# Second chunk's attention in float32 beside the first chunk's first stage, and a reordered opening, in a fused attention and two-MLP kernel

## The chip, the cores and the metric

One core of a Trainium2 chip. The metric is device microseconds (us) of one execution; the time before is the median of three runs. Engines are named as in the profile: PE (TensorE), DVE (VectorE), ACT (ScalarE), POOL (GpSimd), SP (SyncE, which issues most DMAs).

## What is computed

Attention over 4 batches, 8 heads, 576 positions and 64 dimensions, followed by two MLPs of 512 to 2048 to 512 over the 2304 resulting rows. Half of the heads see a local window of 32 positions, half see every 32nd position:

```
scores = where(mask, q @ k.T / 8, -1e9)
attn = exp(scores - max); attn = attn / (sum(attn) + 1e-9)
x = (attn @ v) laid out as [2304, 512]
h = x @ w_in;  x = (h * sigmoid(1.702 h)) @ w_out
h = x @ w2_in; out = (h * sigmoid(h)) @ w2_out
```

q, k and v are float32. The four weights are float64 and are turned into float32 on the chip.

## The kernel before

**Chunks.** The sequence is cut into 8 chunks of 288 positions, two for each batch (an even chunk c has s = 0, an odd one s = 1). For each chunk there is an attention (four head pairs: scores, exponentials, transposes, then two products with v that write x) and the first MLP, in two stages: 16 first-stage tiles (x times a tile of w_in, then gelu) and 64 second-stage steps (times w_out). A first program covers chunks 0 to 6 and the attention of chunk 7; a second covers chunk 7's first MLP and all of the second MLP.

**Precision.** Most products are made of three half-precision products: each operand is scaled and split into a high and a low half (`hi_lo`, L390 high half on ACT or POOL, L395 low half on DVE). The scale needs sums of squares (`square`, L494 on ACT or L496 on DVE, summed by PE at L409). Chunk 0 is the exception: its attention and its MLP run in float32 matmuls without splits, since the weights aren't split yet. A float32 matmul appears in the trace as two instructions.

**Weights.** `convert` (L426) takes a 512 KB float64 tile by DMA (L276, SP's queue) into one of eight landing places or two spare buffers, makes two ACT passes for the parts of the bit pattern (L434, L281), one ACT pass for the sign (L285, into a PSUM bank), one DVE pass (L289) and one POOL addition (L294). Then PE adds the tile to a norm (L302). There are 16 tiles of w_in (into regA) and 16 of w_out (into regB). First-stage tile f of chunk 0 (L829) needs tile f of w_in, second-stage step f (L859) needs tile f of w_out. After chunk 0 has used a tile it is split in place for the later chunks (L832 and L863 are their two stages).

**Order.** All of this is a list of tasks with engines, estimated costs, buffers and a due time (the smaller, the earlier). `Planner.run` plays the list against its own model of engines and one DMA link and fixes the order of instructions on every engine; an engine takes the ready task with the smallest due time, and one that needs another activation table only if none without a switch is due within 24. On the chip the order stands, and each engine waits in it. Chunk 0's MLP is due from 28 (T0), chunk 1's from 86 (T1); the attention of chunk c has its due times relative to the start of chunk c-1 (ATT0 for chunk 0, relative to 0; ATT1 for chunk 1, relative to 28). Weight tile i of w_in is due for loading at 3.0 + 1.9 i, of w_out at 34.0 + 1.9 i.

**Chunk 1 before.** Its q and k are loaded, squared together with chunk 0's k, scaled, and q, both k and v are split; the scores (L681), due from 54, use half-precision operands (kh, qh), and the products with v (L756) use vz and split probabilities (ptt; L720 and L723). There is one buffer each for q (rq), v (rv) and x, two for k (rk).

**Opening before.** Ahead of the plan stand the identity, the masks (mk, made by POOL), the clearing of rv (L348 to L350 on DVE) and of parts of rk. The plan loads chunk 0's q in two DMAs (L567, L568), its k in two (L551, L552), then its v in six (L589), all from SP.

## Time and profile before

| | |
|---|---|
| median of three runs | 862.29 us (859.1 to 863.71) |
| the profiled execution | 863.66 us, of it 861.9 us span |
| PE busy | 817.2 us (95%) |
| DVE, ACT, POOL busy | 629.1 us (73%), 528.2 us (61%), 394.6 us (46%) |
| DMA | 156.86 MB, 182 GB/s over the span |
| chain that ended last | PE 59%, DVE 13%, DMA 9%, ACT 7%, POOL 6%, issue 4% |

The span runs from the first to the last instruction. The chain follows the work that ended last back to its start; "issue" is time in which an engine waited for nothing that the profile shows. In a timeline, a bracket gives the idle time of the engine ahead of the instruction and what ended it. The granted clock is a share of the full 2.4 GHz; its other level is 1.2 GHz.

### The profile page before, as it was taken

The page shows a single profiled execution, that of the slowest core. Times are in us where ns is not written, and L with a number is a line of the kernel's source. Part 1 is how long each engine was busy: PE and PEld are TensorE (multiplying, and loading weights), DVE is VectorE, ACT ScalarE, POOL GpSimd, SP SyncE. Part 2 cuts the span into 40 slices and gives each one's busy share as a digit, 9 for nine tenths or more (in the row PEclk, how much of TensorE's full clock was granted, in tenths as well). Part 3 has the DMA queues.
Part 4 walks back from the last instruction along what each step waited for, and adds up shares of the span by engine and source line. Part 5 has one row for each costly group of instructions (what it writes and reads, how often), then busy time and mean ns, then how long its engine had stood idle before and what let it go on. Part 6 is the DMA issues. An engine that isn't in the chain of part 4 may idle for free.

```text
span 861.9 us, 25035 instructions
## 1 busy us (share of the span) xinstructions
PE 817.2 (95%) x10278; PEld 681.4 (79%) x10278; DVE 629.1 (73%) x1141; ACT 528.2 (61%) x970; POOL 394.6 (46%) x398
## 2 busy tenths in 40 slices
PE   2698899999999998999999999999999999999997
PEld 1575677777788776887878878888889998888886
DVE  5536899965787858988473455879888799878742
ACT  1778878677879569986572434454555576646510
POOL 2638873442442435654321343778877553222110
PEclk9999999999999999999999999999999999999999
DMA  7977724156476386773221652676766889756501
GB/s 163 277 251 208 206 78 133 38 154 183 146 218 221 112 250 200 238 229 115 64 94 36 263 199 83 212 227 223 234 202 217 297 297 307 238 172 233 185 25 50
DMA packets 90227, 156.86 MB, mean 182 GB/s; under 512 B 9032, under 2 KB 48784, under 8 KB 90112
## 3 DMA queue, kind: packets, MB, share of 16 engines
q1 hardware_dynamic: 90112, 155.26, 56.5%
q8 instruction: 80, 1.31, 0.7%
q14 instruction: 35, 0.29, 0.1%
HBM read 101.74 MB, written 53.48 MB: 180 GB/s over the span
## 4 chain that ended last, share of the span: by engine, by line
PE 59%; DVE 13%; DMA 9%; ACT 7%; POOL 6%; issue 4%; SPq 1%; DVEq 0%; POOLq 0%; ACTq 0%
PE aps L1143 9%; PE aps L1254 8%; PE hps L1143 5%; PE gps L1143 4%; PE hps L1254 4%; PE gps L1254 4%; PE aps L863 4%; PE gps L863 3%; DMA rv<-in_v_dram 2%; PE aps L832 2%; DMA regB<-in_moe_w_in_dram 1%; PE gps L1006 1%; PE aps L987 1%; DVE jv L496 1%; DVE regA L395 1%
## 5 line engine op out<-in xcount | busy, mean ns | idle before, releaser
L1143 PEld LDWEIGHTS <-wf 128*128 128x128 f16 x1680 | 150.6, 98 | 15.3
L1254 PEld LDWEIGHTS <-wf 128*128 128x128 f16 x1512 | 147.6, 98 | 18.6 <-issue 1.1
L832 PEld LDWEIGHTS <-regA 128*128 128x128 f16 x1152 | 112.4, 98 | 29.6 <-issue 0.5
L863 PEld LDWEIGHTS <-regB 128*128 128x128 f16 x1152 | 110.6, 99 | 28.0 <-DVE regB L395 0.7
L959 POOL TENSOR_TENSOR tt<-tt 128x256 f32<-128x256 f32 (+2 forms) x84 | 75.7, 912 | 44.0 <-DVE wf L966 11.5
L294 POOL TENSOR_TENSOR wm<-wm 128x512 int32<-128x512 int32 x32 | 43.2, 1349 | 84.6 <-DVE wm L289 66.3
L863 PE MATMUL aps<-g,regB 128*128 128x288 f16 x576 | 78.7, 289 | 0.0
L954 ACT ACTIVATE wf<-tt,xsg 128x512 f16<-128x512 f32 x87 | 58.1, 713 | 27.1 <-PE hps L1254 7.5
L832 PE MATMUL aps<-x,regA 128*128 128x288 f16 x552 | 73.5, 286 | 0.1
L966 DVE SCALAR_TENSOR_TENSOR wf<-tt,xsg,wf 128x512 f16<-128x512 f32 x87 | 70.5, 858 | 0.0
L863 PE MATMUL gps<-g,regB 128*128 128x288 f16 x480 | 64.7, 287 | 0.0
L703 POOL TENSOR_TENSOR prt<-prt,sus 128x378 f32<-128x378 f32 x32 | 28.3, 889 | 58.7 <-DVE sus L702 51.1
L1254 PE MATMUL aps<-regA,wf 128*128 128x256 f16 x456 | 53.2, 273 | 0.1
L1143 PE MATMUL aps<-xfa,wf 128*128 128x256 f16 (+1 forms) x528 | 53.1, 256 | 0.0
L832 PE MATMUL hps<-x,regA 128*128 128x288 f16 x312 | 42.5, 286 | 0.0
L1155 ACT ACTIVATE tt<-tt 128x512 f32<-128x512 f32 x39 | 24.4, 625 | 28.5 <-DVE tt L1150 28.4
L832 PE MATMUL gps<-x,regA 128*128 128x288 f16 x288 | 39.1, 286 | 0.0
L1143 PE MATMUL aps<-g,wf 128*128 128x256 f16 x324 | 38.8, 273 | 0.0
L954 ACT ACTIVATE wf<-regB,xsg 128x512 f16<-128x512 f32 x39 | 27.1, 715 | 18.2 <-DMA regB<-g_scratch 7.0
L1254 PE MATMUL aps<-regB,wf 128*128 128x256 f16 x312 | 37.0, 273 | 0.0
L1254 PE MATMUL hps<-regA,wf 128*128 128x256 f16 x264 | 32.4, 273 | 0.8 <-DVE x L1269 0.5
L966 DVE SCALAR_TENSOR_TENSOR wf<-regB,xsg,wf 128x512 f16<-128x512 f32 x39 | 32.5, 856 | 0.0
(324 smaller groups left out, 1889.7 us busy)
## 6 DMA issues: line engine op xcount, KB each, us to landing
tt<-g_scratch SPq DMA_DIRECT2D x76, 256.0 KB
g_scratch<-tt SPq DMA_DIRECT2D x64, 256.0 KB
w<-in_moe_w_out_dram SPq DMA_DIRECT2D x24, 512.0 KB
regB<-in_moe_w_in_dram SPq DMA_DIRECT2D x16, 512.0 KB
w<-in_moe_w_in_dram SPq DMA_DIRECT2D x16, 512.0 KB
w_scratch<-wm SPq DMA_DIRECT2D x32, 256.0 KB
regB<-g_scratch SPq DMA_DIRECT2D x32, 256.0 KB
wf<-in_factors SPq DMA_DIRECT2D x8, 896.0 KB
```

The lines of the kernel that those rows point to most:

```text
L294: nc.gpsimd.tensor_tensor(out=di, in0=m.bitcast(I32), in1=di, op=ALU.add)
L395: dve_t(n), prio, lambda on: nc.vector.scalar_tensor_tensor(out=lo(), in0=src(), scalar=s(), in1=hi(), op0=ALU.mult, op1=ALU.subtract),
L496: nc.vector.scalar_tensor_tensor(out=jv[:, 0:n], in0=src(), scalar=1.0, in1=src(), op0=ALU.mult, op1=ALU.mult, accum_out=out)
L703: kno = P.add({"POOL": 1.0}, t + 8, lambda on: nc.gpsimd.tensor_tensor(out=sets(N), in0=sets(N), in1=wide(sus[:, sl.idx], 2 * NLB), op=ALU ...
L832: nc.tensor.matmul(o, lhsT=pvA[:, f, x, kk, :], rhs=x1[:, y, kk, :], start=(i == 0), stop=(i == 3 * KD - 1))
L863: nc.tensor.matmul(o, lhsT=pvB[:, f, u, dt * 128:(dt + 1) * 128], rhs=g1[:, w, f, :], start=(f == 0 and j == 0), stop=(f == KF - 1 and j = ...
L954: nc.scalar.activation(out=out, in_=in_, func=AF.Copy, scale=s)
L959: return P.add({e: x for e, x in any_add(n).items() if e in by}, prio, lambda on: (nc.gpsimd if on == "POOL" else nc.vector).tensor_tensor ...
L966: dve_t(n), prio, lambda on: nc.vector.scalar_tensor_tensor(out=lo(), in0=src(), scalar=s(), in1=hi(), op0=ALU.mult, op1=ALU.subtract),
L1143: nc.tensor.matmul(place(b, f), lhsT=wf[:, nf * g + f, x, wa, 128 * kk:128 * kk + 128], rhs=rhs.rearrange("p (h t) -> p h t", h=2) if n2 = ...
L1155: return P.add(act_t(512), t + 5, lambda on: nc.scalar.activation(out=sl(b), in_=sl(b), func=AF.Silu), after, (), [b], tab="silu")
L1254: nc.tensor.matmul(bank(b)[:, 256 * half:256 * half + 256], lhsT=fb[:, x, a, 128 * f:128 * f + 128], rhs=wt[:, 4 * p + f, z, wi, :], start ...
```

## The change

1. Chunk 1's scores and products with v use float32 operands straight from rq, rk and rv, as chunk 0's do. Gone for chunk 1: the squares of q and of both k, the splits of q, both k and v, the split of the probabilities. The squares of v stay and give one scale for x (`small("x1s", ...)`), applied where x is written.
2. Its due times move: load of q and k from 36 to 29, of v from 41 to 37, scores from 54 to 38, products with v from 70 and 84 to 68 and 71. The products with v also wait for all of chunk 0's first-stage tiles, and chunk 1's first-stage tiles for all converted tiles of w_out.
3. Chunk 0's q and k are loaded ahead of everything else, in eight DMAs, half of them issued by ACT: heads 0 and 1 first, then heads 2 and 3. The identity follows them.
4. Chunk 0's v is due for loading at 7.3 in place of 1.0, behind weight tiles 0 to 2 (3.0, 4.9, 6.8).
5. A third of rv's clearing moves from DVE to ACT; an exponential ahead of it loads that table. The planner starts with that table, counts DMA from 2.0 on, and lets no first ACT pass of a w_in tile begin before 13.
6. The strided half of k lies behind the zeros in rk and not ahead of them; chunk 0's products with v are due at 19.2 and 21.0; the reciprocal is due at t + 5.1 in place of t + 7 in every chunk.

The core of the diff:

```diff
+ACT_AT = 13.0
-ATT0 = {"load": (0.0, 1.0), "s": 5.0, "step": 1.5, "av": (12.0, 14.0)}
-ATT1 = {"load": (8.0, 13.0), "square": (14.0, 18.0), "scale": 19.0, "split": (20.0, 21.0, 28.0), "s": 26.0, "step": 6.0,
-        "av": (42.0, 56.0)}
+ATT0 = {"load": (0.0, 7.3), "s": 5.0, "step": 1.5, "av": (19.2, 21.0)}
+ATT1 = {"load": (1.0, 9.0), "square": (0.0, 20.0), "scale": 24.0, "s": 10.0, "step": 6.0, "av": (40.0, 43.0)}
...
-        events, n, link = [], itertools.count(), t
+        events, n, link = [], itertools.count(), t + self.FIRST
...
+    for h in range(0, 4, 2):
+        nq, nk = slice(h * HS, (h + 2) * HS), slice(h * (32 + HS), (h + 2) * (32 + HS))
+        nc.sync.dma_start(out=rq[0:64, nq], in_=q[0][:, nq])
+        nc.scalar.dma_start(out=rq[64:128, nq], in_=q[0][:, NQ:2 * NQ][:, nq])
+        nc.sync.dma_start(out=rk[0:64, 0, nk], in_=k[0][:, nk])
+        nc.scalar.dma_start(out=rk[64:128, 0, KO:NK][:, nq], in_=k[0][:, NK:NK + NQ][:, nq])
...
-    nc.vector.memset(rv[96:128], 0.0)
+    nc.scalar.activation(out=tot[:, 0, 0:1], in_=ones[:, 0:1], func=AF.Exp)
+    nc.scalar.activation(out=rv[96:128].rearrange("p n h d -> p (n h) d"), in_=ones[96:128, None, 0:D].to_broadcast([32, 4 * NV, D]),
+                         func=AF.Copy, scale=0.0)
...
-            out=wm[:, m.idx], in_=raw()[:, :, 1].bitcast(F32), func=AF.Copy, scale=REBIAS), [k0], [m, *dtakes], rb)
+            out=wm[:, m.idx], in_=raw()[:, :, 1].bitcast(F32), func=AF.Copy, scale=REBIAS), [k0], [m, *dtakes], rb, at=act_at)
...
-            sq = [square(c, b + tab["square"][0], NQ, 0, lambda: rq, [kq], [rqb]),
+            sq = [*([square(c, b + tab["square"][0], NQ, 0, lambda: rq, [kq], [rqb])] if c > 1 else []),
...
+        if c > 1:
             qhb, vzb = P.buf("qh"), P.buf("vz")
...
-            if c == 1:
-                split_k(0, b + tab["split"][1])
...
-                            qx = (qh[rows, y] if c else rq[rows])[:, HS * i:HS * i + HS]
+                            qx = (qh[rows, y] if c > 1 else rq[rows])[:, HS * i:HS * i + HS]
...
-            krc = P.add({"DVE": 0.15}, t + 7, lambda on: nc.vector.reciprocal(out=sus[:, sl.idx], in_=sus[:, sl.idx]), [ku], (), [sl])
+            krc = P.add({"DVE": 0.15}, t + 5.1, lambda on: nc.vector.reciprocal(out=sus[:, sl.idx], in_=sus[:, sl.idx]), [ku], (), [sl])
...
-            km = P.add({"PE": 1.4 if c else 2.0}, t, mm, [pts[2 * r][0], pts[2 * r + 1][0], *(k_v if c else [kv])],
-                       pa, [pts[2 * r][1], pts[2 * r + 1][1], rvb if c == 0 else vzb])
+            km = P.add({"PE": 1.4 if c > 1 else 2.0}, t, mm, [pts[2 * r][0], pts[2 * r + 1][0], *(k_v if c > 1 else [kv, *(h_done[0] if c else [])])],
+                       pa, [pts[2 * r][1], pts[2 * r + 1][1], vzb if c > 1 else rvb])
...
-            k = P.add({"PE": 1.95 if c == 0 else 1.47}, t, mm, [*xk, first_in[f] if c == 0 else split_in[f]], [p], [xb])
+            k = P.add({"PE": 1.95 if c == 0 else 1.47}, t, mm, [*xk, first_in[f] if c == 0 else split_in[f], *(first_out if c == 1 else [])], [p], [xb])
...
+    P.FIRST, P.tab = 2.0, "exp"
     P.run()
```

## Rows read from the trace of the kernel before

**Rows 1.** Stage windows: length, busy us of PE, PEld, DVE, ACT, POOL, clock, DMA share, GB/s.
```profile
38.20:83.10 44.90, 41.01 (x255) 30.63 (x253) 25.18 (x36) 32.62 (x62) 27.09 (x16) 0.96 0.73 223
83.10:138.50 55.40, 51.39 (x692) 37.58 (x692) 49.78 (x91) 43.12 (x72) 41.52 (x35) 1.00 0.50 140
...
176.00:478.00 302.00, 293.55 (x4740) 234.91 (x4739) 217.47 (x460) 217.84 (x429) 118.06 (x106) 0.99 0.50 159
478.00:862.00 384.00, 378.41 (x3581) 335.68 (x3578) 282.55 (x437) 187.58 (x316) 179.77 (x196) 1.00 0.61 206
```

**Rows 2.** Windows of 10 us, two of the first ten.
```profile
20.00:30.00 10.00, 4.51 (x90) 3.88 (x90) 3.95 (x10) 7.28 (x15) 4.35 (x5) 1.00 1.03 350
...
70.00:80.00 10.00, 6.15 (x26) 4.16 (x26) 9.67 (x9) 8.35 (x17) 10.00 (x6) 0.86 0.74 234
```

**Rows 3.** The chain in order of time, 10 to 48 us: start, us, what.
```profile
10.86 11.85 DMA regB<-in_moe_w_in_dram
...
30.09 0.83 PE hps L709 x3
...
33.68 2.72 issue
...
38.41 3.95 PE hps L829 x8
...
45.18 2.00 PE gps L829 x8
```

**Rows 4.** Timeline of the opening, all engines: start, us, engine, line, operation.
```profile
8.52 2.29 SPq L589 DMA_DIRECT2D rv<-in_v_dram  x6
...
9.51 0.86 PE L681 MATMUL hps<-rk,rq 64*32 64x63 f32 x42
...
22.72 0.66 ACT L434 ACTIVATE wm<-regB 128x512 f32<-128x512 f32 x1 [9.30 <-DMA regB<-in_moe_w_in_dram]
...
27.10 2.99 PE L756 MATMUL aps<-ptt,rv 64*64 64x32 f32 x84
```

**Rows 5.** Timeline of PE in chunk 0's two stages.
```profile
66.69 1.23 PE L409 MATMUL aps<-tot,ones 128*128 128x1 f32 x10
...
71.35 0.40 PE L302 MATMUL hps<-regA 128*128 128x128 bf16 x4 [1.39 <-POOL regA L294]
...
76.24 0.41 PE L302 MATMUL hps<-regA 128*128 128x128 bf16 x4 [2.50 <-POOL regA L294]
76.49 3.50 PE L829 MATMUL aps<-x,regA 128*128 128x288 f32 x8
...
80.24 0.69 PE L681 MATMUL gps<-kh,qh 64*32 64x63 f16 x60
...
115.37 1.24 PE L756 MATMUL gps<-ptt,vz 64*64 64x32 f16 x120
```

**Rows 6.** Timeline of POOL in the same stretch.
```profile
71.27 2.57 POOL L390 TENSOR_SCALAR kh<-rk,s 128x1280 f16<-128x1280 f32 x1
...
76.17 2.86 POOL L390 TENSOR_SCALAR vz<-rv,s 128x1536 f16<-128x1536 f32 x1
```

**Rows 7.** Waits of PE, 40 to 140 us: us in total, times, longest.
```profile
PE aps L302 <- POOL regB L294: 3.8, 5, 1.5
```

**Rows 8.** Timeline of ACT.
```profile
38.46 1.28 ACT L837 ACT_TABLE_LOAD   x1
...
123.38 1.57 ACT L388 ACTIVATE vz<-rv,s 128x1536 f16<-128x1536 f32 x1
```

**Rows 9.** Windows of 2 us in the opening.
```profile
12.00:14.00 2.00, 2.00 (x89) 1.55 (x87) 2.00 (x8) 0.66 (x2) 0.00 (x0) 1.00 0.54 110
...
24.00:26.00 2.00, 0.51 (x3) 0.50 (x3) 1.18 (x5) 2.00 (x5) 1.39 (x2) 1.00 1.01 414
```

**Rows 10.** Timeline of DVE.
```profile
79.07 2.81 DVE L395 SCALAR_TENSOR_TENSOR vz<-rv,s,vz 128x1536 f16<-128x1536 f32 x1 [0.17 <-POOL vz L390]
```

**Rows 11.** Timeline of SP, the load of chunk 1's v.
```profile
41.98 14.62 SPq L589 DMA_DIRECT2D rv<-in_v_dram  x14
```

More of the change, by code (lines that the diff above doesn't have):

```diff
@@ L607, in scales @@
                 ss, inv = make_scales(banks[bk.idx], len(cols), "a")
-                sx_t[c] = [ss[:, 1:2], inv[:, 1:2]]
+                sx_t[c] = [ss[:, 0:1], inv[:, 0:1]]
+                if c == 1:
+                    sc_t[c] = {"x": small("x1s", ss[:, 0:1], 1.0 / PSC, 1.0)}
+                    return
                 if ks:
@@ L644, in pair @@
             t = b + tab["s"] + tab["step"] * i
-            kb = [k_load[c, "b"], *([k_load[c - 1, "b"]] if s else [])] if c else [kk_t[0]]
+            kb = [k_load[c, "b"], *([k_load[c - 1, "b"]] if s else [])] if c > 1 else [kk_t[x] for x in range(c + 1)]
             def scores(on):
@@ L670, in scores @@
                                 if s == 0:
-                                    kx = (kh[rows, 0, z] if c else rk[rows, kk_t[0].idx])[:, HS * i:HS * i + HS]
+                                    kx = (kh[rows, 0, z] if c > 1 else rk[rows, kk_t[0].idx])[:, KO + HS * i:KO + HS * i + HS]
                                     kx, nk = strided(kx, c0, n), R9 * n
                                 else:
-                                    kx = kh[rows, :, z, HS * i:HS * i + HS].rearrange("p s (c r) -> p c s r", r=R9)[
+                                    assert c > 1 or [kk_t[x].idx for x in range(2)] == [0, 1]
+                                    kx = (kh[rows, :, z] if c > 1 else rk[rows])[:, :, KO + HS * i:KO + HS * i + HS].rearrange("p s (c r) -> p c s r", r=R9)[
                                         :, c0:c0 + n]
@@ L681, in scores @@
                             nc.tensor.matmul(x[0], lhsT=x[1], rhs=x[2], start=False, stop=x[3], skip_group_check=True)
-            ready = [k_q, k_load[c, "s"], *([k_load[c - 1, "s"]] if s else [])] if c else [kq, *k_load[0]]
-            ksc = P.add({"PE": 0.9 if c else 1.8}, t, scores, ready, [*bank, sl], [rqb if c == 0 else qhb, *kb])
+            ready = ([k_q, k_load[c, "s"], *([k_load[c - 1, "s"]] if s else [])] if c > 1 else
+                     [kq, *[y for x in range(c + 1) for y in k_load[x]]])
+            ksc = P.add({"PE": 0.9 if c > 1 else 1.4}, t, scores, ready, [*bank, sl], [qhb if c > 1 else rqb, *kb])
             N = W - 1
@@ L741, in mm @@
                     for e, j, c0, n in BLOCKS[s] if g else [(e, j, 0, 0) for e in range(NLB) for j in range(3)]:
-                        for x, (y, z) in enumerate(HI_LO if c else HI_LO[:1]):
+                        for x, (y, z) in enumerate(HI_LO if c > 1 else HI_LO[:1]):
                             for hh in range(2):
```

54 lines of the change are left out of this document (29 added, 25 removed).

## Prediction, made before the change was run

> **What bounds the kernel now.** I read the busy time by stretches first, then the chain of waits, then the engines' timelines where the chain changes hands. TensorE (PE) is busy 95% of the span, so the question is only where the rest lies and whether work is added to PE. From 478 us on it is busy 378.41 of 384 us, and from 176 to 478 us 293.55 of 302 [rows 1]: whatever shifts the start of chunk 1 shifts the end with it, nearly one for one, because little idle time is left behind it to absorb anything. The idle time that can be had lies ahead of that, in three places.
>
> First, the opening. From 20 to 30 us PE works 4.51 of 10 us [rows 2]. The chain there is one DMA wait of 11.85 us [rows 3]: scores of chunk 0 run from 9.51 us, but ScalarE (ACT) takes the first weight conversion (L434) in its fixed order ahead of the exponentials of two head pairs and stands 9.30 us until that tile lands at 22.72 us. The tile was issued only at 10.86 us, because SP held it behind the load of v (8.52 us, itself behind two clearings of rv). So the product with v starts at 27.10 us [rows 4] and the first-stage tiles at 38.2 us.
>
> Second, two waits for GpSimd (POOL) in the first stage, 1.39 and 2.50 us, and the tile after the second takes 3.50 us [rows 5] where others take 2.00 [rows 3]; the slice has a granted clock of 0.86 [rows 2], so some of it ran at 1.2 instead of 2.4 GHz. POOL is busy all of that slice with halves of chunk 1's k and v between its weight additions [rows 6]. Third, chunk 0's second stage, idle for 4.01 of 55.40 us [rows 1], 3.8 us of it behind POOL's additions [rows 7].
>
> **The change part by part**, against the profiled execution (863.66 us, of it 861.9 span; the median of the runs is 1.4 below).
>
> *Opening.* Eight smaller q and k transfers replace four, on two queues; SP then issues three weight tiles and only then v. One rv clearing goes to ACT: the nearest row is ACT's copy of 1536 elements, 1.57 us [rows 8], so about 3 us for twice as many, after four DMA issues and a table load; it is done before v's turn, and if not, v slips by the excess. The new limit is v. It holds 1.24 MB, and a stretch in which little else moved carried 110 GB/s at a DMA share of 0.54 [rows 9]: 11 us. Ahead of it are q and k (in before the scores at 9.51, [rows 4]; I take 8) and 1.57 MB of weights, 4 us at the 414 GB/s of a good stretch [rows 9], 14 us at 110. So v lands between 18 us (overlapping well) and 27.1 us or later; I take 23, near the sum 8 + 4 + 11, since v is the transfer in front of the wait. The exponentials no longer queue behind a conversion, as conversions may not start before 13 in the plan. **Start of the product with v: -4.1** (0 to -9.1).
>
> Between 27.10 and the end of the first tile at 42.36 us lie two products at 2.99 [rows 4], one tile at 2.00, 0.83 us of transposes of a late head pair, a stall of 2.72 us that the chain calls issue, and a first tile of 3.95 [rows 3], 1.95 over. With all heads ready early the transposes go; the other two have causes that the profile does not show. Of 5.5 I take **-3.5** (0 to -5.5).
>
> *Removed halves and squares.* Chunk 1 no longer needs its q, k and v split: four high halves on POOL, of up to 2.86 us [rows 6], and one on ACT; five low halves on VectorE (DVE), of up to 2.81 us [rows 10], and four of the probabilities; three squares. POOL and DVE are what PE waits for in the first two stages. First stage: the waits and the slow tile, 3.9 + 1.5 = 5.4; I take **-4**, since the additions still need ACT, DVE and a landed tile (0 to -5.4). Second stage: **-2.5** of 4.0; the load order of w_out, which is not changed, keeps the rest (+2 to -4).
>
> *Added on PE.* A float32 score pair takes 0.86 us for its 42 instructions [rows 4], the three half-precision products 0.69 for 60 [rows 5]; four pairs, +0.7. A product with v takes 2.99 us [rows 4] against 1.24 [rows 5]; two, +3.5. Of the ten small sums (1.23 us, [rows 5]) six go, -0.7. **+3.5** (+4.5 if the smaller masked scores do not pack, 0 if they fall in waits that stay). These now stand between first-stage tiles, where PE is the bound, so I charge them. The Trainium skill (FP8 and Floating Point Precision, TensorE Precision Notes) says that true float32 takes four passes through the array; four for three would cost a third more, +1.7 in place of +4.2 before the sums. The rows disagree for the product with v, 2.4 times rather than 1.33, and I keep the rows.
>
> *ACT tables.* Exponentials now fall among the gelus of chunk 0: at least two loads of 1.28 us [rows 8] more at this place. ACT is idle 12.3 of 44.9 us in the first stage [rows 1], and loses one high half and two squares. Cost 0, up to +2.6.
>
> *Later chunks.* The reciprocal's priority moves up for every chunk, and the planner writes a new order for everything up to 478 us. PE's idle time from 176 to 478 us is 8.45 us; I take 0 (-2 to +2). The moved POOL clears keep their size: nothing.
>
> Sum: -4.1 - 3.5 - 4 - 2.5 + 3.5 = -10.6, so 853 for an execution like the profiled one and **852** for the median.
>
> **Rivals.** *The weights set the pace anyway.* The end of chunk 0 hangs on the load and conversion of 32 tiles, not on attention: v lands near 27 us because it now waits for weights, and terms one and two vanish, as do half of the savings behind POOL. For it: DMA share is 1.03 from 20 to 30 us [rows 2]. Against: PE waits for POOL and not for a DMA in the rows of both stages [rows 5, 7]. Time: -3.2 + 3.5, so no change, 862; anything between 858 and 866.6 belongs here (0.5%, or 4.3 us, is what a measurement of this kernel can tell from no change). Chance 0.14.
>
> *SP puts chunk 1's v ahead of the first weights that are still missing.* Its 14 pieces held SP for 14.62 us before [rows 11]. They were due at 41 and tile 13 at 27.7, but rv was free and the eight landing places for weights were not, so they went first, and the last tiles paid with the waits of the first stage. Now rv becomes free when the product with v ends, some 8 us sooner, while the landing places depend on ACT as ever. If v goes while fewer than about four converted tiles are in hand, the first stage stands for up to 14.6 us: -4.1 - 3.5 + 3.5 + 14.6 less the 3.9 us paid already is +6.6, so 869 on the median. Against it: the load is due at 37, after tile 15's 31.5, and conversions begin sooner. Chance 0.09, as **slower**.
>
> *The change gives the whole of the idle time back.* v lands at 18 us, the stall of 2.72 goes, PE waits for POOL nowhere: -9.1 - 5.5 - 5.4 - 4 + 3.5 is -20.5, or 842. It needs every term at its end; chance 0.07, as faster.
>
> That the change does not do what it says could show as chunk 1's scores still running after the first stage, if exponentials keep being put off for want of a table: then the products with v stand in the second stage at float32's price, and the result is that of the first rival.
>
> **How the numbers follow.** Forecast 0.70 (all of it below 858), whole idle time 0.07, weights 0.14, SP 0.09: faster 0.77, same 0.14, slower 0.09. The range 841 to 861 takes in the forecast with its terms pulled either way (v landing five us sooner or four later) and the nearer half of the no-change case; outside lie the slower case and the farther half of no change, and what goes beyond the fullest gain, about 0.2.
>
> **What would show it.** In the new profile: the first conversion on ACT after all four exponentials, and landing well before 22.7 us; the product with v starting near 23 us and released by v's DMA; first-stage tiles from about 29.6 us, at 2.0 to 2.2 us each; score matmuls of 40 float32 instructions between them and no kh, qh or vz for chunk 1; PE busy for more than 41 us in the two stages' idle stretches together, with fewer than 5 us of waits behind POOL; chunk 1's half-precision tiles starting some 10 us sooner. Wrong would be: v landing after 27 us, a stretch with PE idle behind regA additions longer than 4 us in the first stage, more than four table loads before chunk 1, or a gain at chunk 1's start that is given back before 478 us.

## The result, and the profile after

The changed kernel takes 850.28 us (median of four runs, 847.88 to 853.12) against 862.42 of the kernel before in the same comparison: ratio 0.9866, 95% interval 0.9822 to 0.9911. The forecast was 852 in a range of 841 to 861, with 0.77 on faster. The profiled execution took 851.69 us, 849.9 of it span, 12.0 less span than before. PE is busy 814.95 us, 2.2 less than before.

The number came out right, and most of the reasons did not. Five marks in the two traces show where the 12 us arose. The first mark is the start of the first instruction of its kind on PE, the others are the end of the last:

| | before | after | difference |
|---|---|---|---|
| first-stage tiles of chunk 0 begin | 38.2 | 29.0 | -9.2 |
| first stage of chunk 0 ends | 83.3 | 74.2 | -9.1 |
| second stage of chunk 0 ends | 139.0 | 136.5 | -2.5 |
| second stage of chunk 1 ends | 199.5 | 195.5 | -4.0 |
| second stage of chunk 6 ends | 478.0 | 466.0 | -12.0 |
| span ends | 861.9 | 849.9 | -12.0 |

So the opening gained over nine microseconds, chunk 0's second stage gave 6.6 of them back, and eight new ones arose between chunks 1 and 6, where the forecast had put nothing. Every mark is from one execution of each kernel. The windows between the marks, of the kernel after; the columns are those of [rows 1]:

```profile
0.00:29.00 29.00, 15.67 (x373) 12.54 (x373) 14.81 (x37) 15.78 (x26) 12.47 (x29) 1.00 0.91 248
29.00:74.20 45.20, 42.19 (x371) 31.87 (x369) 21.34 (x55) 40.14 (x75) 20.77 (x19) 0.96 0.78 236
74.20:136.50 62.30, 53.19 (x482) 39.81 (x479) 49.51 (x77) 41.19 (x67) 40.57 (x30) 0.92 0.51 149
136.50:195.50 59.00, 59.00 (x1003) 47.77 (x1001) 49.79 (x104) 42.04 (x85) 23.64 (x23) 1.00 0.38 120
195.50:466.00 270.50, 266.52 (x4319) 214.97 (x4317) 201.47 (x411) 204.04 (x415) 109.98 (x101) 1.00 0.50 161
466.00:849.90 383.90, 378.38 (x3580) 335.69 (x3578) 281.27 (x437) 187.17 (x316) 176.09 (x196) 1.00 0.61 206
```

Read the first number behind the length (PE) against the length. The second stage (third row) is 62.3 us long with 9.1 idle; before, it was 55.7 by the marks, with 4.0 idle. So of the 6.6 us that it lost 5.1 are idle time, and 1.5 are busy time of PE, at a lower clock (0.92 against 1.00). The last row is the second program and is the same in both kernels, 383.9.

**The opening.** Timeline of the kernel after, chosen rows:

```profile
3.56 1.55 SPq L276 DMA_DIRECT2D regB<-in_moe_w_in_dram  x3
5.79 4.21 SPq L601 DMA_DIRECT2D rv<-in_v_dram  x6
8.41 0.52 ACT L713 ACTIVATE prt<-prt 128x378 f32<-128x378 f32 x1 [0.88 <-DVE prt L710]
10.12 0.65 ACT L444 ACTIVATE wm<-regB 128x512 f32<-128x512 f32 x1
13.61 0.51 ACT L713 ACTIVATE prt<-prt 128x378 f32<-128x378 f32 x1
19.79 1.08 PE L772 MATMUL aps<-ptt,rv 64*64 64x27 f32 x32 [4.27 <-DMA rv<-in_v_dram]
23.28 1.04 PE L772 MATMUL aps<-ptt,rv 64*64 64x18 f32 x16 [0.48 <-DMA rv<-in_v_dram]
26.58 2.21 PE L772 MATMUL gps<-ptt,rv 64*64 64x32 f32 x84
28.97 2.15 PE L846 MATMUL hps<-x,regA 128*128 128x288 f32 x8
```

The weights are issued at 3.56 us and not at 10.86 [rows 3], ACT takes the first of them at 10.12 with no wait ahead of it, where it stood 9.30 us [rows 4], and the last exponential starts at 13.61. The product with v then works through v as its pieces land: its last 16 instructions wait for the last piece, at 23.28. The first tile takes 2.15 us in place of 3.95 [rows 3]. The last is partly luck of the execution: in the ten kernels with the new opening the first tile takes 2.15 us twice and 3.23 to 4.15 us eight times. Its start is the safer mark: 28.9 to 30.9 us in those ten, 34.9 to 38.2 in the four kernels with the old opening.

**The second stage.** ACT, SP and PE of the kernel after, from the first stage into the second:

```profile
37.24 15.87 SPq L601 DMA_DIRECT2D rv<-in_v_dram  x14
51.09 1.28 ACT L713 ACT_TABLE_LOAD   x1
57.30 1.28 ACT L854 ACT_TABLE_LOAD   x1
62.17 0.61 PE L302 MATMUL hps<-regA 128*128 128x128 bf16 x4 [2.09 <-POOL regA L294]
82.40 1.28 ACT L713 ACT_TABLE_LOAD   x1
83.69 0.93 ACT L713 ACTIVATE prt<-prt 128x378 f32<-128x378 f32 x2
94.91 1.48 PE L772 MATMUL aps<-ptt,rv 64*64 64x32 f32 x80
95.96 2.17 SPq L601 DMA_DIRECT2D rv<-in_v_dram  x6
109.73 0.45 PE L419 MATMUL aps<-tot,ones 128*128 128x1 f32 x2 [2.64 <-ACT jk L504]
110.65 1.86 PE L419 MATMUL aps<-tot,ones 128*128 128x1 f32 x8 [0.46 <-DVE jv L506]
```

Chunk 1's first two exponentials get their table at 51.09. The other two are put off until 82.40. So the second product with chunk 1's v runs at 94.91, and rv is in use until then. SP loads chunk 2's v from 95.96, and PE stands at the sums of that v's squares until 109.73. SP's own waits, asked for from 95 to 97 us (us in total, times, longest), show what held the load:

```profile
SPq L276 <- ACT regB L281: 7.7, 1, 7.7
SPq L601 <- PE aps L772: 0.9, 1, 0.9
```

The order put the load behind three w_out tiles on SP (80.84 to 95.17 us), and the last of them stood 7.7 us until ACT had read an older tile out of its place. The product with v added 0.9 us. So it is the planned order, written for a late product, that delays v; freeing rv sooner without a new order would have gained less than a microsecond there. The chain of waits of the kernel after has this load in its row `97.76 11.04`:

```profile
9.73 13.50 DMA rv<-in_v_dram
97.76 11.04 DMA rv<-in_v_dram
```

The waits of PE from 30 to 150 us (us in total, times, longest) name the rest of the second stage's idle time, additions of w_out tiles, 5.9 us where they were 3.8 [rows 7]; with the 2.6 and 0.5 at the sums that makes 9.0 of the 9.1:

```profile
PE hps L302 <- POOL regB L294: 5.9, 3, 2.8
PE aps L419 <- ACT jk L504: 2.6, 1, 2.6
PE hps L302 <- POOL regA L294: 2.6, 3, 2.1
```

And the clock fell with it. Windows of the kernel after, the last three columns being clock, DMA share and GB/s:

```profile
102.00:110.00 8.00, 3.91 (x20) 2.53 (x18) 3.41 (x4) 2.43 (x4) 3.08 (x3) 0.99 0.85 199
112.00:114.00 2.00, 2.00 (x7) 1.57 (x7) 1.31 (x7) 2.00 (x4) 0.69 (x2) 0.50 0.74 262
```

PE works 3.91 of 8 us, and then runs at 0.50, its lower level of 1.2 GHz: a pair of w_out matmuls takes 1.31 us at 112.37 and 0.70 at 104.93.

### The profile page after: what moved, and what is told of

Same layout as the page of the kernel before. It is cut to its first block, busy times and chain, and to the rows that moved or that the text cites. A ratio compares the mean times of both kernels' runs of the same rounds, so it can differ in the third digit from the quotient of the medians.

```text
span 849.9 us, 24691 instructions
## 1 busy us (share of the span) xinstructions
PE 814.9 (96%) x10112; PEld 682.7 (80%) x10112; DVE 618.2 (73%) x1118; ACT 530.4 (62%) x980; POOL 383.5 (45%) x396
## 4 chain that ended last, share of the span: by engine, by line
PE 68%; DMA 15%; DVE 5%; ACT 5%; POOL 3%; issue 2%; SPq 1%; DVEq 0%; POOLq 0%; ACTq 0%
PE aps L1161 10%; PE aps L1272 8%; DMA rv<-in_v_dram 7%; PE hps L1161 5%; PE aps L849 4%; PE gps L1161 4%; PE gps L880 4%; PE aps L880 4%; PE hps L1272 4%; PE gps L1272 4%; DMA regB<-in_moe_w_in_dram 2%; PE gps L849 2%; PE hps L880 2%; PE hps L849 2%; PE gps L1024 1%
## 5 line engine op out<-in xcount | busy, mean ns | idle before, releaser
L977 POOL TENSOR_TENSOR tt<-tt 128x256 f32<-128x256 f32 (+2 forms) x84 | 75.2, 905 | 45.4 <-ACT tt L1173 12.1
L849 PE MATMUL aps<-x,regA 128*128 128x288 f16 x624 | 83.0, 286 | 0.0
L294 POOL TENSOR_TENSOR wm<-wm 128x512 int32<-128x512 int32 x32 | 45.9, 1438 | 68.1 <-DVE wm L289 63.0
L880 PE MATMUL aps<-g,regB 128*128 128x288 f16 x432 | 58.9, 286 | 0.0
L880 PE MATMUL gps<-g,regB 128*128 128x288 f16 x384 | 52.2, 286 | 0.0
L880 PE MATMUL hps<-g,regB 128*128 128x288 f16 x336 | 44.7, 286 | 0.0
L1173 ACT ACTIVATE tt<-tt 128x512 f32<-128x512 f32 x39 | 24.4, 625 | 30.5 <-DVE tt L1168 30.3
L405 DVE SCALAR_TENSOR_TENSOR g<-aps,sg,g 128x288 f16<-128x288 f32 x52 | 26.2, 512 | 17.0 <-ACT g L398 16.7
L289 DVE SCALAR_TENSOR_TENSOR wm<-wm,aps 128x512 int32<-128x512 int32 x35 | 23.8, 681 | 15.5 <-ACT aps L285 15.5
```

What stands on the lines that cost most here:

```text
L289: nc.vector.scalar_tensor_tensor(out=mi, in0=mi, scalar=3, in1=ri, op0=ALU.logical_shift_left, op1=ALU.bitwise_or)
L294: nc.gpsimd.tensor_tensor(out=di, in0=m.bitcast(I32), in1=di, op=ALU.add)
L405: dve_t(n), prio, lambda on: nc.vector.scalar_tensor_tensor(out=lo(), in0=src(), scalar=s(), in1=hi(), op0=ALU.mult, op1=ALU.subtract),
L849: nc.tensor.matmul(o, lhsT=pvA[:, f, x, kk, :], rhs=x1[:, y, kk, :], start=(i == 0), stop=(i == 3 * KD - 1))
L880: nc.tensor.matmul(o, lhsT=pvB[:, f, u, dt * 128:(dt + 1) * 128], rhs=g1[:, w, f, :], start=(f == 0 and j == 0), stop=(f == KF - 1 and j = ...
L977: return P.add({e: x for e, x in any_add(n).items() if e in by}, prio, lambda on: (nc.gpsimd if on == "POOL" else nc.vector).tensor_tensor ...
```

## The experiments

All twelve stand here, with the two kernels themselves. "First tile", "stage 2", "chunk 1" and "chunk 6" are the marks of the table above; the last column is the time from chunk 1's end to chunk 6's end. Marks come from one profiled execution, medians and ratios from all runs of the kernel; a ratio is to the runs of the kernel before in the same comparison, whose medians were 860.95 to 862.42. Two kernels whose order on PE is the same (after and one_queue) differ by 1.5 us in the last column, so a difference of that size says nothing. The expectations count a chunk's end from the start of its last group of second-stage steps, which lies 1.6 us before the mark for chunk 1 (193.9 for 195.5 in the changed kernel, 197.9 for 199.5 before) and 6.0 for chunk 6, and a stretch "to the end" ends 4.7 us before the span's end.

| kernel | median us | ratio to before (95%) | first tile | stage 2 | chunk 1 | chunk 6 | 1 to 6 |
|---|---|---|---|---|---|---|---|
| before | 862.42 | | 38.2 | 139.0 | 199.5 | 478.0 | 278.5 |
| after | 850.28 | 0.9866 (0.9822 to 0.9911) | 29.0 | 136.5 | 195.5 | 466.0 | 270.5 |
| opening_only | 858.56 | 0.9946 (0.9927 to 0.9965) | 30.4 | 136.2 | 196.3 | 472.7 | 276.4 |
| f32_only | 857.64 | 0.9943 (0.9918 to 0.9969) | 34.9 | 137.7 | 195.8 | 471.0 | 275.2 |
| recip_only | 871.31 | 1.0102 (1.0066 to 1.0139) | 35.4 | 140.2 | 205.2 | 485.9 | 280.7 |
| recip_back | 860.82 | 1.0003 (0.9973 to 1.0034) | 28.9 | 134.0 | 192.9 | 471.9 | 279.0 |
| one_queue | 853.90 | 0.9922 (0.9892 to 0.9952) | 29.2 | 137.2 | 196.2 | 468.2 | 272.0 |
| v_first | 856.17 | one run | 30.2 | 135.4 | 194.4 | 470.5 | 276.1 |
| act_at_0 | 857.16 | 0.9942 (0.9910 to 0.9975) | 29.2 | 135.0 | 193.2 | 472.6 | 279.4 |
| v_in_vz | 863.21 | 1.0018 (0.9991 to 1.0044) | 30.9 | 148.3 | 203.2 | 478.6 | 275.4 |
| exps_once | 849.06 | 0.9857 (0.9807 to 0.9907) | 29.8 | 128.7 | 188.0 | 461.5 | 273.5 |
| park_after | 853.26 | 0.9925 (0.9900 to 0.9949) | 30.5 | 134.0 | 192.9 | 468.1 | 275.2 |
| fact_after | 854.00 | 0.9906 (0.9873 to 0.9939) | 30.9 | 139.3 | 198.3 | 470.5 | 272.2 |
| park_before | 864.50 | 1.0024 (0.9997 to 1.0050) | 37.4 | 137.3 | 198.3 | 482.1 | 283.8 |

### The parts alone

**opening_only**: the kernel before with the opening of the change (its points 3 to 5 and chunk 0's due times), the attention of chunk 1 as before.

```diff
-ATT0 = {"load": (0.0, 1.0), "s": 5.0, "step": 1.5, "av": (12.0, 14.0)}
+ATT0 = {"load": (0.0, 7.3), "s": 5.0, "step": 1.5, "av": (19.2, 21.0)}
...
+    for h in range(0, 4, 2):
...
+    P.FIRST, P.tab = 2.0, "exp"
```

> Only the opening of the change (two queues, v behind three weight tiles, clearing on ACT, first conversion not before 13); chunk 1's attention stays in split halves, the reciprocal stays at t + 7. Forecast's theory (the opening is worth over half of the gain): the first first-stage tile of chunk 0 ends near 31 us as in the changed kernel (42.4 before), chunk 1's last second-stage step starts 4 us or more sooner than before (197.9), and the median is 5 to 8 us below before, about 855. Rival (the head start is given back at the wait for the second and third chunk's operands, the gain comes from the order of later chunks): same first tile, under 2 us left at chunk 1's last step, and a total that follows whatever the later chunks do, 855 to 864.

The result lies between theory and rival. The first tile ends at 33.6 us (30.40 + 3.23) and not near 31, chunk 1's last step starts 3.3 us sooner, and the median is 3.0 us below before. Of the 7.8 us that the first tile starts sooner, 2.8 are left at the end of the second stage, although chunk 1 still has its half-precision attention: PE waits here 2.6 us for DVE's split of k, 2.3 for POOL's additions in regA and 2.2 for a step of the softmax on DVE.

**f32_only**: the kernel before with chunk 1's attention in float32 and its due times, the opening and the reciprocal as before.

```diff
-        "av": (42.0, 56.0)}
+ATT1 = {"load": (1.0, 9.0), "square": (0.0, 20.0), "scale": 24.0, "s": 10.0, "step": 6.0, "av": (40.0, 43.0)}
...
+        if c > 1:
             qhb, vzb = P.buf("qh"), P.buf("vz")
```

> Only chunk 1's float32 attention with its new due times; opening and reciprocal as before. Forecast's theory: the first tile ends at 42.4 as before, PE waits for POOL in the two stages fall by 3 to 6 us and 3.5 us of PE work are added, so chunk 1's last second-stage step is within 3 us of 197.9 and the median within 3 us of before, 859 to 865. Rival (the head start is worth little, the lighter DVE and POOL in chunks 1 to 4 bring the gain): 5 us or more below before, under 857, with the gain behind 198 us.

Both sizes were missed: chunk 1's last step starts 3.8 us sooner (194.1) and the median is 3.9 us below before, outside the theory's 3 and short of the rival's 5. This run has the waits of the changed kernel's second stage without the new opening: 3.1 us at the sums of chunk 2's squares and 5.3 for regB, with chunk 2's v issued at 101.36 (88.95 before). They belong to the float32 half with its due times.

**recip_only**: the kernel before with the reciprocal's due time alone; **recip_back**: the changed kernel without it.

```diff
-            krc = P.add({"DVE": 0.15}, t + 7, ...
+            krc = P.add({"DVE": 0.15}, t + 5.1, ...
```

> The kernel before with only the reciprocal's due time at t + 5.1 in every chunk. Theory that the earlier reciprocal frees the transposes and brings what is gained behind 198 us: chunk 1's last step near 198, chunk 6's last step 6 to 9 us sooner than 472, median 853 to 857. Rival (any new order of the later chunks shifts their waits by some us either way): within 4 us of before, either sign, 858 to 866.

> The changed kernel with the reciprocal back at t + 7. Theory that the earlier reciprocal brings the later gain: 856 to 859, with chunk 1's last step near 194 as in the changed kernel and chunk 6's last step near 468. Rival (order of later chunks): 846 to 855, either side of 850.

Neither expectation of recip_only (853 to 857 and 858 to 866) nor of recip_back (856 to 859 and 846 to 855) was met. Measured against the 861.54 of before in that comparison: the opening gave 3.0 us, float32 3.9, the reciprocal alone cost 9.8. Their sum is +2.9, the whole change gave -12.1: the parts don't add. The same edit of 1.9 in one due time costs 9.8 us in the kernel before, and in the changed kernel it gains 10.5 (860.82 without it, 850.28 with it, in two comparisons). The 9.8 do not lie in the opening: recip_only's first tile begins 2.8 us sooner than before's, though the granted clock was 0.79 in its first 30 us, and its chunk 1 ends 5.7 us later. Recip_back is ahead of the changed kernel by 2.6 us at chunk 1's end and behind it by 5.9 at chunk 6's. Neither size fits one reciprocal of 0.15 us; what the edit also changes is the order that the planner writes behind it. Which place of that order costs the time stays open.

### What gained the opening

**one_queue**: all eight q and k loads from SP.

```diff
-        nc.scalar.dma_start(out=rq[64:128, nq], in_=q[0][:, NQ:2 * NQ][:, nq])
+        nc.sync.dma_start(out=rq[64:128, nq], in_=q[0][:, NQ:2 * NQ][:, nq])
...
-        nc.scalar.dma_start(out=rk[64:128, 0, KO:NK][:, nq], in_=k[0][:, NK:NK + NQ][:, nq])
+        nc.sync.dma_start(out=rk[64:128, 0, KO:NK][:, nq], in_=k[0][:, NK:NK + NQ][:, nq])
```

> The changed kernel with all eight first q and k transfers issued by SP; PE's order is the same. Theory that two queues matter little, since four issues of 0.6 us end about when the bytes do: scores start at most 1.5 us later (7.8 for 6.3), the first weight tile lands 2 to 3 us later because SP issues it after eight transfers (6.1 for 3.6), the product with v is released by v's DMA within 2 us of 19.8, the median within 3 us of the changed kernel. Rival (the second queue is what lets weights and v start early): first-stage tiles start 3 us or more after 29.0, median 853 or more.

The first weight tile is issued at 5.86 us in place of 3.56, and the first tile starts at 29.2 in place of 29.0: the second queue is worth nothing that shows at this mark, as the theory has it. (The median is 3.6 us above the changed kernel's with the same order on PE, a little more than the 3 allowed; the profiled execution's granted clock was 0.77 over the first 30 us, and it lost 0.7 by chunk 1's end and 1.5 more by chunk 6's.) The Trainium skill (DMA: Bandwidth & Descriptors, Issuing engines are not separate DMA queues) says that starting transfers from several engines saves only the time to issue them; this run agrees.

**v_first**: v is due for loading at 1.0 again, ahead of the weights.

```diff
-ATT0 = {"load": (0.0, 7.3), "s": 5.0, "step": 1.5, "av": (19.2, 21.0)}
+ATT0 = {"load": (0.0, 1.0), "s": 5.0, "step": 1.5, "av": (19.2, 21.0)}
```

> The changed kernel with chunk 0's v due at 1.0, ahead of the weight tiles, as before. Theory that v is the transfer which ends the wait ahead of the products: v lands 4 to 6 us sooner (by 16 us), the product with v is done by 22 us, but the first conversion on ACT waits for its tile until 18 us or later, so that the first-stage tiles start within 2 us of 29.0. Rival (v's place is what brought the opening's gain): first-stage tiles start at 32 us or later, chunk 1's last step at 196 or later.

Its first tile starts at 30.2, 1.2 later, as the theory has it. Which of v and the weights goes first is worth about a microsecond there, by one run.

**act_at_0**: conversions may start at any planned time.

```diff
-ACT_AT = 13.0
+ACT_AT = 0.0
```

> The changed kernel with ACT_AT = 0 in place of 13: the plan may put a first ACT pass of a weight tile at any time. Nothing is left out. The first conversion then stands ahead of all four exponentials of chunk 0 on ACT, as two of them stood behind it in the kernel before; the first weight tile is still issued at about 3.6 us. Theory 1 (the opening was gained because the tile now lands at 9.7 and not at 22.7 us): ACT waits about 1 us for the tile, the exponentials run from 10 to 16 us, the product with v still waits for v's DMA, the first tile starts at 29 to 31. Theory 2 (it was gained by the order on ACT, as the prediction has it): the exponentials are late again by 5 us or more and the first tile starts at 33 or later. The rest of the order is written anew as well, so the total says little: 848 to 858.

Timeline of act_at_0:

```profile
9.58 0.66 ACT L444 ACTIVATE wm<-regB 128x512 f32<-128x512 f32 x1 [2.05 <-DMA regB<-in_moe_w_in_dram]
10.70 0.50 ACT L713 ACTIVATE prt<-prt 128x378 f32<-128x378 f32 x1
15.41 0.52 ACT L713 ACTIVATE prt<-prt 128x378 f32<-128x378 f32 x1
25.49 2.98 PE L772 MATMUL gps<-ptt,rv 64*64 64x32 f32 x84
29.23 4.15 PE L846 MATMUL hps<-x,regA 128*128 128x288 f32 x8
```

The first conversion now stands ahead of all four exponentials, waits 2.05 us for its tile and delays the last exponential by 1.80 us; the first tile starts at 29.2 all the same, as theory 1 has it. It is the early landing of the tile, not the bar on conversions, that freed the exponentials. In the total the run lost 6.9 us against the changed kernel's median; in the profiled executions all of the loss is behind chunk 1, whose end is even 2.3 us earlier.

So of the 9.2 us that the first tile starts sooner, one queue, v ahead of the weights and the bar on conversions, each undone alone, take back 0.2 to 1.2. Of the rest of the opening (smaller loads of q and k ahead of everything, the table loaded early, the clearing on ACT, the planner's start) no run undoes one part, and some of it is order: f32_only and recip_only, with the old opening, start 3 us sooner than before too. Which part carries the gain stays open.

### What lost the second stage

**v_in_vz**: chunk 1's v goes into the memory of vz, which is free then, so that rv is free early for chunk 2's v. POOL clears that memory first.

```diff
+    vzf = vz.rearrange("p a n d -> p (a n d)").bitcast(F32).rearrange("p (n h d) -> p n h d", n=NV, h=4)
...
+    nc.gpsimd.memset(vzf, 0.0)
...
-        rqb, rvb = P.buf("rq"), P.buf("rv")
+        rqb, rvb = P.buf("rq"), P.buf("vz" if c == 1 else "rv")
```

> The changed kernel, with chunk 1's v loaded into the memory of vz (12 KB in each partition, unused until chunk 2's split) in place of rv, cleared once by POOL. Theory that the head start of chunk 0's first stage is given back because chunk 2's v can't be loaded before the second product with v of chunk 1 has freed rv (load issued at 96 us, landed 108.8, PE idle 3.1 us at L409's sums and clock 0.66 after): the load is issued before 80 us, the wait at the sums goes, chunk 0's last second-stage step ends 4 to 7 us sooner than 136.5 and chunk 1's last step starts at 187 to 190 in place of 193.9. Rival (POOL's additions of w_out set the pace of the second stage in any case): ends at 134 to 137, chunk 1's last step within 2 us of 193.9. The total goes with the later chunks' order on top of that: 844 to 860.

Windows and timeline of v_in_vz:

```profile
30.90:82.90 52.00, 45.10 (x366) 33.66 (x364) 25.51 (x57) 35.28 (x65) 19.69 (x16) 0.93 0.89 232
82.90:148.30 65.40, 57.19 (x638) 43.39 (x638) 58.90 (x95) 47.04 (x82) 48.48 (x38) 0.92 0.47 141
```

```profile
26.29 12.85 SPq L604 DMA_DIRECT2D vz<-in_v_dram  x13
52.18 1.26 POOL L294 TENSOR_TENSOR regA<-wm,regA 128x512 int32<-128x512 int32 x1 [12.00 <-DVE wm L289]
```

The wait at the sums of chunk 2's v is gone, as it had to be, but both stages are longer than in the changed kernel, and neither theory nor rival was met (the second stage ends at 148.3). With a free buffer the planner put chunk 1's v on SP from 24.48 us on (the row shows 13 of its 14 pieces), ahead of the eight weight tiles of w_in still missing, and chunk 2's v at 43.66 ahead of the last four. POOL stood 12.00 us without a tile to add, and PE waited for regA up to 3.4 us. That is the second rival of the forecast, and this is its price: a first stage of 52.0 us in place of 45.2. The run says nothing clean about the second stage, so it was tried in another way.

**exps_once**: chunk 1's four scores are due 1.0 apart and not 6.0.

```diff
-ATT1 = {"load": (1.0, 9.0), "square": (0.0, 20.0), "scale": 24.0, "s": 10.0, "step": 6.0, "av": (40.0, 43.0)}
+ATT1 = {"load": (1.0, 9.0), "square": (0.0, 20.0), "scale": 24.0, "s": 10.0, "step": 1.0, "av": (40.0, 43.0)}
```

> The changed kernel with chunk 1's scores due 1.0 apart (38, 39, 40, 41) and not 6.0 apart. In the planned order all four exponentials of chunk 1 then stand in one visit to the exponential table, between gelus of the first stage, and SP's load of chunk 2's v stands four weight tiles earlier. Nothing is left out. Theory (the head start is lost in the second stage because two exponentials are put off to 83.7 us, so that rv is free only at 96.4 and chunk 2's v lands at 108.8): both products with v stand before 80 us, chunk 2's v is issued before 85, the 3.1 us at the sums of v's squares are gone, chunk 0's second stage ends near 132 in place of 136.5, chunk 1's first half-precision tile starts at 120 to 122 in place of 125.2. Rival (the second stage is paced by landing and conversion of w_out whatever v does): its end stays at 136 to 137 and regB waits grow to 8 or more. The total is 846 to 849 by the theory if what follows chunk 1 takes the 651 us that it took in the changed kernel, and up to 857 if the new order takes the 661 of the worst one.

Timeline and windows of exps_once:

```profile
48.26 1.28 ACT L713 ACT_TABLE_LOAD   x1
53.10 0.91 ACT L713 ACTIVATE prt<-prt 128x378 f32<-128x378 f32 x2
59.07 1.28 ACT L854 ACT_TABLE_LOAD   x1
77.87 2.34 SPq L601 DMA_DIRECT2D rv<-in_v_dram  x6
93.16 1.05 PE L419 MATMUL hps<-tot,ones 128*128 128x1 f32 x8 [1.30 <-DVE jv L506]
```

```profile
74.30:128.70 54.40, 49.47 (x537) 37.03 (x536) 49.31 (x74) 44.77 (x77) 45.38 (x33) 0.97 0.63 187
188.00:461.50 273.50, 267.55 (x4430) 214.68 (x4429) 207.05 (x434) 207.07 (x411) 115.24 (x102) 1.00 0.50 163
```

One visit to the table holds all four, chunk 2's v is issued 18.1 us sooner (77.87 against 95.96), and the second stage takes 54.4 us in place of 62.3. This is the theory's result, and better: the stage ends at 128.7, and chunk 1 ends 7.5 us ahead of the changed kernel. The stage is 1.3 us below the 55.7 of before, half of the 2.5 that the forecast had wanted of it. At chunk 6 the lead is 4.5. The median of 849.06 can't be told from the changed kernel's 850.28; the profiled execution was 4.6 us shorter, but it is the shortest of its kernel's four.

The run does not take the late v alone out. PE's waits at the sums fell from 3.1 to 1.3 us and those for regB from 5.9 to 2.1, its busy time fell by 3.7, and the w_out tiles have other places on SP as well. Shown is that the place of these exponentials in the plan costs the 8 us of the second stage. Not shown is how they divide between the late v and the tiles of w_out.

### What gained the later chunks

**park_after** and **park_before** move one constant by 1 us, in the changed kernel and in the kernel before: the due times of the conversions of the second MLP's weights, which the first program makes and writes out for the second. What park_before's expectation calls the splitting of chunk 0's used tiles is this same constant.

```diff
-PARK = (160.0, 6.0)
+PARK = (161.0, 6.0)
```

> The changed kernel with one number moved: the conversions of the second MLP's weights (PARK) are due 1 us later in the plan, 161 for 160. No operation is added or removed and the plan of the first two chunks' attention stays. Theory that the 8 us gained between chunk 1's and chunk 6's last second-stage steps (265.9 us from one to the other, against 274.1 before and 275.1 to 278.5 in the four partial kernels) are one favourable order among many: the stretch goes to 272 to 279 and the median to 856 to 862, though the reason for the gain was not touched. Rival (the three parts together take real work or waits out of the later chunks): the stretch stays at 264 to 269 and the median at 848 to 853.

> The kernel before with one constant moved: the splitting of chunk 0's used weight tiles is due from 161 in place of 160. Nothing is left out; the order on PE is the same up to some 125 us and written anew behind that. Theory (the 8 us gained behind chunk 1 belong to the order that the planner happens to write, not to anything that the change does there): the same work in another order takes other times, so the stretch from chunk 1's last second-stage step to the end, 659.4 us in the kernel before, moves by 2 us or more either way (651 to 661 was seen over nine orders), and the total with it, to 853 to 864. Rival (the late gain is a property of the change, the order matters little): the stretch stays at 658 to 661, total within 2 us of 861.

**fact_after** moves another by 2 us, in the changed kernel (the due times of a later step on the same weights); PE's order differs from about 258 us on.

```diff
-FACT = (270.0, 21.0)
+FACT = (272.0, 21.0)
```

> The changed kernel with one constant moved: FACT's first due time is 272 in place of 270. Nothing is left out; PE's order is the same up to about 258 us. Theory (order by chance): up to chunk 1's last second-stage step all as in the changed kernel (193.9), and the rest, 651.3 there, becomes 652 to 658, total 851 to 857, since the changed kernel had the shortest of nine orders. Rival (a gain that the change makes for good): rest 650 to 652, total within 1.5 us of 850.3.

The same work took 5.3 us more between chunks 1 and 6 in park_before than in the kernel before (283.8 against 278.5), and 4.7 more in park_after than in the changed kernel (275.2 against 270.5). By the expectation's count park_after has 270.7, between the theory's 272 to 279 and the rival's 264 to 269, and its median of 853.26 lies between theirs too. Park_before moved by more than 2 us, as the theory has it, but its median of 864.50 is above both ranges. Its profiled execution (868.87) is the slowest of its ten, and its ratio of 1.0024 can't be told from no change: its 5.3 is one execution's.

Fact_after shows less, 272.2, 1.7 more; its rest by the count of the expectation is 653.0, within the theory's 652 to 658 but hardly beyond what one_queue shows without any new order on PE (272.0). Its profiled execution is 4.5 us longer than the changed kernel's, and 2.8 of that is there at chunk 1's end, where the order is still the same; 1.9 of the 2.8 is there when the first tile starts, behind a stretch at the granted clock of 0.50 (see the last section). So a new order behind 258 us alone did little in this one case.

What makes the changed kernel's stretch the shortest can be read from PE's busy and idle time in it. After, PE is busy 266.52 of 270.50 us (the row 195.50:466.00 above); before, 270.33 of 278.50:

```profile
199.50:478.00 278.50, 270.33 (x4381) 216.48 (x4379) 204.01 (x436) 203.34 (x403) 108.31 (x100) 0.99 0.50 159
```

So the 8.0 us are 4.2 less idle and 3.8 less busy. The largest wait of PE in the stretch, before and then after:

```profile
PE aps L709 <- POOL prt L703: 1.7, 3, 0.7
PE aps L725 <- POOL prt L719: 2.7, 3, 1.4
```

Both are waits for POOL's step of a later chunk's softmax; before, six other groups of waits make up the rest, after, 1.1 us of "issue". How much idle time there is goes with the order: park_after has 7.8 us of idle time in the stretch, park_before 11.5. Of the busy time a small part only changed sides of the mark (62 of 4381 recorded matmuls fewer in the stretch after); in one slice before, from 285 to 290 us, the granted clock was 0.66, behind 1.57 us in which PE stood.

Over the fourteen kernels the column runs from 270.5 to 283.8. The four orders with half-precision attention in chunk 1 (before, opening_only, recip_only, park_before) have 276.4 to 283.8, in the mean 279.9; the seven with float32 attention and an order of their own (f32_only, recip_back, v_first, act_at_0, v_in_vz, exps_once, park_after) have 273.5 to 279.4, in the mean 276.3; the changed kernel's order has 270.5 and 272.0 in two kernels. Shown is, in one execution each, that one constant moved by 1 us moves this stretch by some 5, in either kernel, against 1.5 for one order in two kernels, and that the changed kernel has the shortest of them. Not shown is how much of the eight belongs to the change in any order: the means differ by 3.6, but the two sets overlap, and no run held the order fixed.

## Why the prediction was right, and where it wasn't

The forecast's terms against the marks, the opening counted to the end of the first tile:

| | forecast | measured |
|---|---|---|
| opening | -7.6 | -11.2 |
| rest of the first stage, with the float32 work | -0.5 | +2.1 |
| second stage | -2.5 | +6.6 |
| chunk 1's second stage | 0 | -1.5 |
| later chunks | 0 | -8.0 |
| sum | -10.6 | -12.0 |

**Opening, -4.1 and -3.5: right in kind, too small.** The end of the first tile moved from 42.36 [rows 3] to 31.12 us (28.97 + 2.15), -11.2 in place of -7.6. That v lands at 23 was met (9.73 + 13.50 = 23.23 in the chain). The step that failed: the product was taken to start when all of v is in; it starts with the pieces at 14.37 and 19.79, and only its last 16 instructions wait for 23.28. The stated reason, that conversions may not start before 13, failed too: two conversions stand between the exponentials, and act_at_0, with one ahead of them all, starts the tiles at 29.2. Of the 5.5 us behind the product's start the stall of 2.72 went and the first tile lost 1.80, though that pace came in two of ten executions only. The transposes did not go: two groups of three stand between the products, from 24.25 to 25.80. The rest of the surplus is the products themselves, of which 68 instructions had run before v was all in and the second of which took 2.21 us for its 84 instructions, where the row of before has 2.99.

**Added on PE, +3.5: mis-sized, near zero.** A product with chunk 1's v takes 1.48 us (the row at 94.91 above) against 1.24 for the three half-precision products [rows 5]. A pair's 40 score instructions take 0.64 us and not 0.86, against 0.69 for the 60 of before [rows 5]:

```profile
70.97 0.64 PE L696 MATMUL aps<-rk,rq 64*32 64x63 f32 x40
```

That makes 2 x 0.24 - 4 x 0.05 - 0.7 = -0.4. The row that the prediction took, 2.99 us [rows 4], stood in the opening, where the same instructions run at half their later pace. By the Trainium skill (FP8 and Floating Point Precision, TensorE Precision Notes), with four passes for true float32, a product would have cost an estimated 1.65 us, four thirds of 1.24. The prediction kept the row and weighed this away; the 1.48 of the trace of after lies much nearer to the page.

**First stage, -4 with the float32 work inside it.** It was to be half a microsecond shorter (-4 + 3.5) and is 45.2 long against 45.1, or 2.1 longer behind its first tile. Both terms were smaller: PE waits 2.6 us for regA in place of 3.9, and the tile behind the longest wait is as slow as before (3.50 [rows 5]), at a granted clock of 0.60 from 62.50 to 66.30:

```profile
62.57 3.63 PE L846 MATMUL gps<-x,regA 128*128 128x288 f32 x8
```

So of the 5.4 us that the term counted 1.3 went, not 4. SP issued the last four tiles only at 53.20, behind the 15.87 us of chunk 1's v, and ACT then stood 1.84 us for that v, and had its squares and a table load to do before the next tile was converted. The mechanism of the second rival was there, at a price of some 2 us (the wait of 2.09) and not of 14.6. Besides, the stage now holds four pairs of scores where it held one (80.24 [rows 5]); the other three stood in the second stage.

**Second stage, -2.5: wrong by 9 us.** It is 6.6 us longer (62.3 against 55.7). The step that failed is "ACT tables: 0", and with it the -2.5, which took the waits behind POOL to fall: they rose from 3.8 to 5.9 us. The loads cost little time themselves; what the sum left out is that the planner puts exponentials off for want of a table, and that the product behind them uses rv, so that the order puts chunk 2's load, its squares and PE's sums late. The forecast named the put-off exponentials, but only as a way in which the change might fail as a whole. Exps_once shows where the loss lies: with one table visit the stage takes 54.4.

**Later chunks, 0 (-2 to +2): -8.** The bound was the step that failed. It was taken from PE's idle time of 8.45 us, as if that were all that a new order could move, and by a guess at that. Half of the idle time went (8.2 to 4.0 us from chunk 1's end to chunk 6's), and PE's busy time fell by 3.8 as well. Three runs with one constant shifted moved the stretch by 1.7, 4.7 and 5.3 us. Nothing in the forecast made the order written here the shortest of those seen; that part is luck, as far as these runs show.

**The rivals.** The weights did not set the pace in the opening, SP's order cost 2 us, and idle time was not all given back. The forecast was right on the sign and the size because errors of 9.1 and 2.6 us met errors of 3.6, 1.5 and 8.0 the other way. Its list of signs caught this: "more than four table loads before chunk 1" was on it as wrong, and there are five (3.26, 33.64, 51.09, 57.30 and 82.40 us; three before). Waits behind POOL in the two stages are 8.9 us and not under 5 (2.6 for regA, 5.9 for regB, 0.4 for probabilities), and chunk 1's half-precision tiles started 2.4 us sooner (125.2 against 127.6), not 10. The gain was given back ahead of chunk 1, and not behind it as the last sign has it.

## What to carry to other kernels

Where a planner or a list scheduler writes the order, price an edit together with the order that it causes: shift one due time by a microsecond or two in both kernels and see how far the time moves. Here a shift of 1 us moved one stretch by some 5 us in single executions and the medians by about 3, which is hardly clear of noise, and a shift of 1.9 moved the medians by some 10 us, more than any part of the change did alone.

A table switch can be paid for in what waits behind the work that is put off, more than in the 1.28 us of the load: group the work that needs the other table, follow the buffer that its last user frees, and look at what the issuing queue has ahead of the load that wants that buffer.

Take an operation's price from a place like the one it will stand in; a row from a kernel's first 40 us can be twice the price.

## What the runs showed of the hardware

**The opening's pace differs between executions, and the clock column does not always show it.** The same 84 float32 instructions and the tile behind them, in fact_after, whose order is the changed kernel's there:

```profile
27.79 2.77 PE L772 MATMUL gps<-ptt,rv 64*64 64x32 f32 x84
30.89 3.70 PE L846 MATMUL hps<-x,regA 128*128 128x288 f32 x8
```

and its window at that place:

```profile
26.00:30.00 4.00, 4.00 (x91) 3.74 (x90) 1.87 (x4) 3.29 (x7) 1.89 (x2) 0.50 1.01 271
```

At the granted clock of 0.50 they take 2.77 and 3.70 us; in the kernel after, 2.21 and 2.15 at 1.00. Fact_after's first tile starts 1.9 us behind the changed kernel's, and its first chunks stay behind. Act_at_0 takes 2.98 and 4.15, as long as at 0.50, but its window reads 1.00:

```profile
26.00:30.00 4.00, 4.00 (x92) 3.81 (x88) 1.69 (x3) 3.33 (x8) 1.27 (x1) 1.00 1.03 336
```

The kernel before has the same pair of numbers, 2.99 [rows 4] and 3.95 [rows 3], and the clock of its slice from 20 to 30 us reads 1.00 [rows 2]. That its first tile of 3.95 was a tile at 1.2 GHz is likely, but argued from durations alone. The Trainium skill (TensorE: Matmul & The Clock Gate, Part 1) warns that these clock events have been seen to be unreliable; durations of like instructions are the better witness here.

**One load, several landings.** The product with v ran its first 68 instructions while the last piece of v was still on its way; it waited 4.27, 0.86 and 0.48 us for three of the pieces. One time for a load of several transfers was too coarse a price.
